# Loading the keys of the last unit but one in two halves (attention of one query row over a long cache, one core)

## The chip, the cores and the metric

The kernel runs on one core of one Trainium2 chip. The metric is the device time of one execution in microseconds (us), the median of several runs. Five engines work side by side, each with an instruction queue of its own: TensorE (PE in the profile, its weight loads PEld), VectorE (DVE), ScalarE (ACT), GpSimd (POOL) and SyncE (SP), which here only issues transfers between the main memory and the on-chip buffers (DMA). Engines and transfers meet through semaphores.

## The reference

Decoding attention with grouped queries: 32 query heads share 8 heads of keys and values. There is one query row for each head, and the cache is 65536 positions long with 128 numbers each, all in bf16. K and V hold 134 MB each and are read once.

```python
B, Hq, Hkv, Sq, Sk, D = 1, 32, 8, 1, 65536, 128
k = jnp.repeat(k, Hq // Hkv, axis=1)
v = jnp.repeat(v, Hq // Hkv, axis=1)
scores = jnp.einsum("bhqd,bhkd->bhqk", q, k) * D ** -0.5
p = softmax(scores, axis=-1)
return jnp.einsum("bhqk,bhkd->bhqd", p, v)
```

## The kernel before

**Units.** Each head of keys is cut into 4 units of 16384 positions, so there are NU = 32 units, numbered 0 to 31. A unit lies in a buffer as 128 partitions by T = 128 columns of 128 numbers, 32 KB in each partition and 4 MB in all. There are two buffers for keys, `kbuf[0]` for even and `kbuf[1]` for odd units, and one buffer `vbuf` that holds the values of two units.

**Rounds.** TensorE runs a loop of NR = 16 rounds of two units, a = 2i and b = 2i + 1: keys of a, keys of b, values of a, values of b. In the last round the values of b, unit 31, come after the loop, in `pe_last`.

**Keys** (`pe_keys`). The 128 columns are taken in G = 16 groups of 8. TensorE transposes the 8 columns of a group into one of four PSUM buffers `trb` (line 136). VectorE (line 229) or, for every fourth group, ScalarE (line 227) copies them to `ktb` in the on-chip memory. TensorE multiplies them with the 4 queries of the head into the scores `qkb` (line 147). The scores follow the transposes three groups behind (LAG = 3), so a unit opens with the transposes of four groups, 32 in a row. Before column 0 TensorE takes 16 from the semaphore `krdy` of the buffer, before column HALF = 64 it takes 16 from `khalf`:

```python
if t == 0:
    take(pe, krdy[b], 16)
if t == HALF:
    take(pe, khalf[b], 16)
```

**Softmax.** When the scores of a unit are done, VectorE finds their maximum over the columns (line 256), GpSimd the one over the partitions, VectorE the new running maximum, and ScalarE the exponentials `pts` (line 369), after which TensorE may use them.

**Values** (`value`, line 166). 128 multiplications of a column block of V with `pts` add up in `pvb`; VectorE adds the result to `acc`. After the second unit of a round VectorE increments `vfree` (line 310), which allows SyncE to fill `vbuf` again.

**The end** (`pe_last`). The values of unit 31 arrive in six pieces of 64, 32, 16, 10, 4 and 2 columns with a semaphore each. The first 126 columns go through line 166, in two runs of 64 and 62 that a small product (line 187) parts, the last two columns through line 196, and line 200 adds what was summed before. VectorE scales the result (line 357) and SyncE stores it (line 444).

**The order of the transfers.** SyncE issues everything in the order of its program: in round i the keys of unit 2i (after `kfree[0]`), those of 2i + 1 (after `kfree[1]`), then both units' values (after `vfree`). An eviction of the last group of a unit frees its key buffer. A unit's keys are one transfer that increments `krdy`; SyncE itself then adds 16 to `khalf` (lines 432 and 433), so that the wait at column 64 passes. For units 0 and 31 the keys are two transfers of 64 columns each, one increments `krdy`, the other `khalf` (line 430, with the issue in line 422). In the last round the values of unit 30 are one transfer (line 442), and those of unit 31 are the six pieces (line 443, issued by line 422).

## Time and profile before

| | |
|---|---|
| time, median of 3 runs | 633.53 us (633.5 to 633.71) |
| the profiled execution: time / span | 633.8 us / 632.0 us |
| mean granted clock of TensorE over the span | 0.789 |
| busy: PE / DVE / ACT / POOL | 77% / 49% / 29% / 3% |
| data read | 268.44 MB, 425 GB/s over the span |

The span runs from the first to the last instruction; the time has what lies around it as well. In rows of the timeline the first number is the start from the beginning of the span, the second the duration, both in us; merged rows stand for several instructions (x32). A bracket at the end of a row gives the idle time of that engine before it and what ended it; "PEq L41" means that TensorE's own queue released it, at the helper that waits for a semaphore (line 41). "SPq" are issues by SyncE's queue. "PEclk" is the share of full clock that TensorE was granted.

### The profile page before, as it was taken

How to read it: one execution, taken by the hardware profiler on the slowest of the kernel's cores; microseconds unless marked ns; L12 is line 12 of the kernel's file. 1: busy time of each engine (PE TensorE's matmuls, PEld its weight loads, DVE VectorE, ACT ScalarE, POOL GpSimd, SP SyncE). 2: the span in 40 equal slices, each digit the busy share in tenths (PEclk: the TensorE clock that was granted, in tenths of full speed). 3: DMA queues.
4: the chain of work that ended last, by engine and by line, in shares of the span. 5: the costliest groups of instructions: out<-in, count | busy, mean ns of one | idle time of the engine just before them, and what ended most of it. 6: DMA issues, size and time to landing. Idle time of an engine off the chain costs nothing. (4 is left out here: it accounts for less than half of the span.)

```text
span 632.0 us, 26791 instructions
## 1 busy us (share of the span) xinstructions
PE 489.4 (77%) x12294; PEld 482.3 (76%) x12294; DVE 312.0 (49%) x689; ACT 185.6 (29%) x410; POOL 15.9 (3%) x49
## 2 busy tenths in 40 slices
PE   4858869687796768968689497895968869687698
PEld 4858869687796768968689496885968869687697
DVE  4634627346272562725637165461744717356173
ACT  1321414214142240412414124141431414214142
POOL 0000000000000000000000000000000000000000
PEclk9866959769596895968969688695976959769596
DMA  8999999999999999999999999999999999999995
GB/s 367 450 418 444 428 425 442 433 446 419 431 448 415 448 415 431 448 415 448 415 431 452 413 450 417 450 428 417 450 423 456 415 431 452 417 450 412 417 431 203
DMA packets 8174, 268.61 MB, mean 425 GB/s; under 512 B 994, under 2 KB 1250, under 8 KB 1506
## 3 DMA queue, kind: packets, MB, share of 16 engines
q1 hardware_dynamic: 8072, 268.44, 98.7%
q8 instruction: 7, 0.11, 0.1%
q14 instruction: 5, 0.04, 0.0%
q10 hardware_dynamic: 90, 0.02, 0.0%
HBM read 268.44 MB, written 0.01 MB: 425 GB/s over the span
## 5 line engine op out<-in xcount | busy, mean ns | idle before, releaser
L136 PE MATMUL trb<-ident,kbuf 128*128 128x128 bf16 x4096 | 328.5, 233 | 41.3 <-PEq L41 41.3
L229 DVE COPY ktb<-trb 128x1024 bf16<-128x1024 bf16 x384 | 254.1, 689 | 101.0 <-PE trb L136 97.8
L136 PEld LDWEIGHTS trb<-ident,kbuf 128*128 128x128 bf16 x4096 | 263.1, 105 | 42.3 <-issue 42.2
L227 ACT ACTIVATE ktb<-trb 128x1024 bf16<-128x1024 bf16 x128 | 131.0, 1023 | 384.9 <-PE trb L136 324.8
L147 PE MATMUL qkb<-qcur,ktb 128*128 128x4 bf16 x4096 | 170.7, 165 | 22.7 <-PEq L41 21.9
L147 PEld LDWEIGHTS qkb<-qcur,ktb 128*128 128x128 bf16 x4096 | 153.2, 97 | 26.7 <-issue 23.9
L166 PE MATMUL pvb<-pts,vbuf 128*128 128x4 bf16 x4094 | 111.9, 166 | 71.6 <-PEq L41 68.7
L166 PEld LDWEIGHTS pvb<-pts,vbuf 128*128 128x128 bf16 x4094 | 110.8, 104 | 72.9 <-issue 72.9
L369 ACT ACTIVATE pts<-qkb,negm 128x128 bf16<-128x128 f32 x128 | 50.5, 540 | 0.9
L256 DVE TENSOR_REDUCE cmax<-qkb 128x4 f32<-128x512 f32 x32 | 22.1, 692 | 44.7 <-DVEq L41 43.7
L369 ACT ACTIVATION_READ_ACCUMULATOR pts<-qkb,negm 128x1 f32 x128 | 34.6, 270 | 0.0
L291 DVE TENSOR_TENSOR acc<-acc,pvb 128x4 f32<-128x4 f32 x23 | 3.6, 158 | 62.3 <-DVEq L41 62.3
L407 POOL PARTITION_ALL_REDUCE cmaxa<-cmax x32 | 11.9, 371 | 580.6 <-POOLq L41 580.6
L276 DVE TENSOR_TENSOR lp<-lp,alpha 128x4 f32<-128x4 f32 x24 | 3.8, 159 | 34.2 <-DVEq L41 34.2
L365 ACT ACTIVATE alpha<-dm 128x4 f32<-128x4 f32 x24 | 4.9, 205 | 52.6 <-ACTq L41 52.6
L289 DVE COPY acc<-pvb 128x4 f32<-128x4 f32 x8 | 1.3, 162 | 29.7 <-DVEq L41 29.7
L266 DVE TENSOR_TENSOR m<-m,cmaxa 128x4 f32<-128x4 f32 x24 | 3.8, 159 | 11.5 <-DVEq L41 11.5
L238 DVE COPY qcur<-qT 128x4 bf16<-128x4 bf16 x8 | 1.4, 170 | 11.8 <-DVEq L41 11.6
L283 DVE TENSOR_TENSOR acc<-acc,alpha 128x4 f32<-128x4 f32 x24 | 3.9, 163 | 4.2 <-DVEq L41 1.7
L267 DVE TENSOR_TENSOR dm<-m 128x4 f32<-128x4 f32 x24 | 3.9, 162 | 3.5
L277 DVE TENSOR_TENSOR lp<-lp,rsum 128x4 f32<-128x4 f32 x24 | 3.9, 162 | 3.5
L207 PE MATMUL trb<-ident,qsb 32*128 32x32 bf16 x1 | 0.2, 204 | 5.0 <-DMA qsb<-in_q_dram 5.0
(43 smaller groups left out, 26.8 us busy)
## 6 DMA issues: line engine op xcount, KB each, us to landing
kbuf<-in_k_dram SPq DMA_DIRECT2D x30, 4096.0 KB, 26.3
kbuf<-in_k_dram SPq DMA_DIRECT2D x4, 2048.0 KB, 16.0
vbuf<-in_v_dram SPq DMA_DIRECT2D x1, 4096.0 KB, 21.4
vbuf<-in_v_dram SPq DMA_DIRECT2D x1, 2048.0 KB, 26.0
vbuf<-in_v_dram SPq DMA_DIRECT2D x1, 1024.0 KB, 28.0
vbuf<-in_v_dram SPq DMA_DIRECT2D x1, 512.0 KB, 28.8
vbuf<-in_v_dram SPq DMA_DIRECT2D x1, 320.0 KB, 29.1
vbuf<-in_v_dram SPq DMA_DIRECT2D x15, 31.0
```

The source lines that it names most:

```text
L136: ins = pe.transpose(trb[j % NTB][:, i * P:(i + 1) * P], kv[:, t, :], ident[:, :])
L147: ins = pe.matmul(qkb[b][:, t * R:(t + 1) * R], lhsT=ktb[:, off:off + P], rhs=qcur[:, :], start=True, stop=True)
L166: return pe.matmul(pvb[b][:, 0:R], lhsT=vv[:, b * T + t, :], rhs=pts[b][:, t * R:(t + 1) * R], start=t == first, stop=t == last)
L227: ins = e.activation(dst, trb[j % NTB][:, :], AF.Copy).then_inc(eva, 1)
L229: ins = e.tensor_copy(dst, trb[j % NTB][:, :]).then_inc(evd, 1)
L256: e.tensor_reduce(cmax[:, :], qkb[u % 2][:, :].rearrange("p (t g) -> p g t", g=R), AX.X, ALU.max).then_inc(cm, 1)
L267: e.tensor_tensor(dm[:, :], mo[:, :], mn[:, :], ALU.subtract)
L277: own(e, e.tensor_tensor(lp[:, :], lp[:, :], rsum[:, :], ALU.add), xd)
L283: own(e, e.tensor_tensor(acc[:, :], acc[:, :], alpha[u % 2][:, :], ALU.mult), xd)
L365: e.activation(alpha[u % 2][:, :], dm[:, :], AF.Exp, scale=scale)
L369: ins = e.activation(pv[:, g, :], sv[:, g, :], AF.Exp, bias=negm[:, g:g + 1], scale=scale, accum_out=rsum[:, g:g + 1])
L407: e.partition_all_reduce(cmaxa[:, :], cmax[:, :], P, bass.bass_isa.ReduceOp.max).then_inc(cma, 1)
```

## The change

The condition in `load_k` that picks the units whose keys come as two transfers now names unit 30 (NU - 2) as well as 0 and 31:

```diff
             b = n % 2
             if n >= 2:
                 e.wait_ge(kfree[b], n // 2)
-            if n in (0, NU - 1):
+            if n in (0, NU - 2, NU - 1):
                 pieces(kbuf[b], src(kf, n), (HALF, T - HALF), (krdy[b], khalf[b]))
             else:
                 e.dma_start(kbuf[b][:, :], src(kf, n)).then_inc(krdy[b], 16)
                 e.sem_inc(khalf[b], 16)
```

For unit 30 one transfer of 4096 KB becomes two of 2048 KB, columns 0 to 63 and 64 to 127. The first increments `krdy[0]`, the second `khalf[0]`, and SyncE's own increment of `khalf[0]` is left out for this unit. Nothing else changes.

## The prediction

> **What bounds the kernel now.** I read the page first, then the list of DMA transfers, and last the merged timeline of the final 50 us. Two lines of the page say what rules most of the time:

> ```profile
> span 632.0 us, 26791 instructions
> q1 hardware_dynamic: 8072, 268.44, 98.7%
> ```

> The transfers of K and V keep the 16 DMA engines busy for 98.7% of the span. The change removes no bytes, so it can pay only where the program stops being held by the stream: at its end. The timeline of the end, rows of TensorE (PE), VectorE (DVE) and the SyncE queue (SPq); columns are start, duration, engine, line, operation, tiles, count, and in brackets the idle time before:

> ```profile
> 569.66 0.33 SPq L432 DMA_DIRECT2D kbuf<-in_k_dram  x1
> 580.94 0.81 SPq L422 DMA_DIRECT2D kbuf<-in_k_dram  x2
> 586.98 6.97 PE L166 MATMUL pvb<-pts,vbuf 128*128 128x4 bf16 x256 [4.48 <-PEq L41]
> 594.43 0.33 SPq L442 DMA_DIRECT2D vbuf<-in_v_dram  x1
> 594.80 2.81 SPq L422 DMA_DIRECT2D vbuf<-in_v_dram  x6
> 596.50 3.57 PE L136 MATMUL trb<-ident,kbuf 128*128 128x128 bf16 x32 [2.56 <-PEq L41]
> 603.00 0.61 PE L136 MATMUL trb<-ident,kbuf 128*128 128x128 bf16 x8
> 609.70 1.95 PE L136 MATMUL trb<-ident,kbuf 128*128 128x128 bf16 x32
> 621.24 3.55 PE L166 MATMUL pvb<-pts,vbuf 128*128 128x4 bf16 x128
> 625.46 1.85 PE L166 MATMUL pvb<-pts,vbuf 128*128 128x4 bf16 x64 [0.38 <-PEq L41]
> 627.36 1.82 PE L166 MATMUL pvb<-pts,vbuf 128*128 128x4 bf16 x62
> 629.11 0.37 PE L196 MATMUL pvb<-vbuf,pts 128*4 128x128 bf16 x2
> 630.05 0.34 DVE L357 TENSOR_SCALAR olast<-pvb,rl 4x128 bf16<-4x128 f32 x1 [0.68 <-PE pvb L200]
> ```

> Read downwards, this is: values of units 28 and 29 (586.98), a gap of 2.56 us, keys of unit 30 (596.50), keys of unit 31 (609.70), values of unit 30 (621.24), values of unit 31 in three rows (625.46, 627.36, 629.11), and the output. From 596.50 on TensorE and the engines that serve it hardly pause. To see whether that stretch waits for data, the issues are set beside the times to landing (last column, us from issue), first K of unit 30 and the two halves of K of unit 31, then V of unit 30 and the six pieces of V of unit 31:

> ```profile
> kbuf<-in_k_dram SPq DMA_DIRECT2D x1, 4096.0 KB, 26.7
> kbuf<-in_k_dram SPq DMA_DIRECT2D x1, 2048.0 KB, 20.3
> kbuf<-in_k_dram SPq DMA_DIRECT2D x1, 2048.0 KB, 24.8
> ...
> vbuf<-in_v_dram SPq DMA_DIRECT2D x1, 4096.0 KB, 21.4
> vbuf<-in_v_dram SPq DMA_DIRECT2D x1, 2048.0 KB, 26.0
> vbuf<-in_v_dram SPq DMA_DIRECT2D x1, 1024.0 KB, 28.0
> vbuf<-in_v_dram SPq DMA_DIRECT2D x1, 512.0 KB, 28.8
> vbuf<-in_v_dram SPq DMA_DIRECT2D x1, 320.0 KB, 29.1
> vbuf<-in_v_dram SPq DMA_DIRECT2D x1, 128.0 KB, 29.0
> vbuf<-in_v_dram SPq DMA_DIRECT2D x1, 64.0 KB, 28.7
> ```

> K of unit 30 lands at 569.66 + 26.7 = 596.4, some 0.1 us before its first transpose at 596.50: this landing ends the gap. K of unit 31 lands at 580.94 + 20.3 = 601.2 and 581.35 + 24.8 = 606.2 (the two issues fill 0.81 us, 0.41 each), before 609.70. V of unit 30 lands at 615.8, before 621.24. The six pieces are issued 0.476 us apart (2.81 us less a last issue of 0.43, over 5), from 594.80 to 597.18, and land at 620.8, 623.3, 624.6, 625.3, 625.7 and 625.9. They are used from 625.46, 627.4, 628.3, 628.8, 629.1 and 629.11 (29 ns for each column, from 62 in 1.82 us). Each is early; the last has the least to spare, 629.11 - 625.9 = 3.2 us. So the end of this kernel is a chain of TensorE work that starts with the landing of unit 30's keys and is not held by any later transfer.

> **The change, part by part.** *The first transpose of unit 30.* The keys arrive as two transfers of 2048 KB, and the first 64 columns release TensorE. The halves of unit 31 landed 606.2 - 601.2 = 5.0 us apart, so I put the first half of unit 30 at 596.4 - 5.0 = 591.4. TensorE is then still in the values of unit 29, which end at 586.98 + 6.97 = 593.95. What is late next is thus TensorE itself and the turn of its loop. That turn is seen uncovered once, in the second round, where the keys had long landed:

> ```profile
> 50.84 2.72 PE L166 MATMUL pvb<-pts,vbuf 128*128 128x4 bf16 x96 [2.85 <-issue]
> 53.61 3.57 PE L136 MATMUL trb<-ident,kbuf 128*128 128x128 bf16 x32
> ```

> From 53.56 to 53.61 are 0.05 us. The keys of unit 30 therefore start at 594.00 in place of 596.50: 2.50 us.

> *The second half.* TensorE now waits for a real landing at column 64, the first of the group of eight transposes at 603.00. That is 6.5 us after the start, so about 600.3 in the changed kernel, against a landing at 596.4: about 4 us to spare. Queued behind that wait are the other transposes of the unit, and behind them the evictions on VectorE and ScalarE; none is held.

> *The clock within unit 30.* TensorE starts these keys at half clock. The table of stretches (columns: stretch, length, busy time and count for PE, PEld, DVE, ACT, POOL, then PEclk, DMA share, GB/s) shows when it changes:

> ```profile
> 211.60:211.70 0.10, 0.10 (x6) 0.10 (x4) 0.09 (x1) 0.00 (x0) 0.00 (x0) 0.80 0.00 0
> 583.60:583.80 0.20, 0.00 (x0) 0.00 (x0) 0.00 (x0) 0.00 (x0) 0.17 (x1) 0.73 0.76 328
> 587.00:593.90 6.90, 6.90 (x256) 6.86 (x256) 0.48 (x3) 0.00 (x0) 0.00 (x0) 0.50 0.93 401
> 600.70:600.80 0.10, 0.10 (x4) 0.10 (x2) 0.00 (x0) 0.10 (x1) 0.00 (x0) 0.70 1.16 492
> 621.20:621.30 0.10, 0.10 (x7) 0.09 (x4) 0.00 (x0) 0.00 (x0) 0.00 (x0) 0.70 1.70 696
> ```

> A mean of 0.70 in 0.1 us between the levels 0.50 and 1.00 places an edge: up at 211.64, down at 583.69, up at 600.76, down at 621.24. The distances 17.07 and 20.48 are 5 and 6 times 3.414 us, so I read the edges as lying on a grid of that step. Unit 30 ran cold for 600.76 - 596.50 = 4.26 us. With a start at 594.00 the next grid point is 597.35, 3.35 us later. A round with almost that delay exists, unit 10, which starts at 208.24 and turns warm 3.40 us later; its rows, and the first one of unit 11:

> ```profile
> 208.24 3.55 PE L136 MATMUL trb<-ident,kbuf 128*128 128x128 bf16 x32 [2.59 <-PEq L41]
> ...
> 221.12 1.05 PE L136 MATMUL trb<-ident,kbuf 128*128 128x128 bf16 x16
> ```

> It takes 221.12 - 208.24 = 12.88 us from its keys to the next ones, where unit 30 took 609.70 - 596.50 = 13.20. That gives another 0.32 us, and a slope of 0.32 / 0.86 = 0.37 us for each us of cold time. If the grid lies otherwise in another execution, the delay can be as long as two steps, 6.8 us, which would cost 0.37 x 2.5 = 0.94 us instead: the gain lies between 1.6 and, with a delay a little shorter, 3.0.

> The row 587.00:593.90 holds more: TensorE is fully busy with values and stays at 0.50. [...]

> *The queue.* One more issue on SyncE, 0.41 us at 570.0, stands in front of nothing: the next, for unit 31, goes out at 580.94 when its buffer is free, and unit 30's own data land 26.7 us after the issue because other transfers are ahead. The increment of the second semaphore by SyncE goes away. The release of V's buffer comes from VectorE after the values of unit 29, which do not move, so V is issued at 594.43 as before. The price of the split on the stream is bounded by unit 31, whose halves took 606.2 - 596.4 = 9.8 us, and V of unit 30, one transfer, 615.8 - 606.2 = 9.6 us: up to 0.2 us later for V of unit 31. Below nothing there is no room, since the bytes are the same. I take 0.1.

> [...]

> *The sum.* 2.50 + 0.32 = 2.82 us, if nothing behind it is late. Keys of unit 31 start at 594.00 + 12.88 = 606.9, after both landings. Values of unit 30 start at 618.4, after 615.8. Values of unit 31 start at 622.6 (landed 620.8), reach column 64 at 624.5 (623.3), and the last two columns at 626.3, against 625.9 + 0.1. The stretch from 609.70 on moves as a whole, with 0.3 us left. The span goes from 632.0 to 629.2; the profiled execution took 633.8 us, 1.8 more than its span, and would take 631.0. The median of the three runs, 633.53, lies 0.27 below the profiled one, so the median of the changed kernel is 633.53 - 2.82 = 630.7 us.

> **The rivals.** [...]

> *The stream stops between the halves.* A transfer on an empty queue shows how long that could be:

> ```profile
> DMA to landing us min/median/max: 7.3/27.0/29.1
> ```

> The shortest landing of line 422 is 7.3 us, for 2048 KB that take 4.9 us in the stream (half of 9.8). The other 2.4 us are what would be lost if the second half only began when the first had been confirmed. V of unit 31 would then be complete at 628.3, 0.8 us before 629.11, so the gain shrinks to 0.8: 632.7 us. Against it stand the halves of unit 31, 5.0 us apart.

> *Nothing happens.* If the gap of 2.56 us were the turn of the loop, which the bracket <-PEq L41 (its own queue) does not exclude, an earlier landing would not start anything: 633.5. The same follows if the first half landed only with the second, by engines that do not keep to the order. Against these stand the 0.05 us at 53.56 and the halves of unit 31.

> *Slower.* The split halves the contiguous run of each partition. In the stretch where V's small pieces are moved the rate is low:

> ```profile
> 623.00:625.00 2.00, 2.00 (x69) 1.78 (x65) 0.24 (x3) 1.49 (x9) 0.00 (x0) 0.50 0.61 221
> ```

> At 221 GB/s the 4.19 MB of unit 30 would take 19.0 us instead of 9.7, and all later landings would move back by 9.3. The last piece of V would come at 635.2, 6.1 us after its use at 629.11: 639.6 us. This mechanism decides from a delay of 3.2 us on, below which V stays hidden even against the old end. Against it: unit 31 has runs of the same length and moves at the full rate.

> **How the numbers follow.** The forecast has a chance of 0.84, the warm clock 0.05, the stop between halves 0.04, nothing 0.05, slower 0.02. About 0.2%, 1.27 us, is what a measurement of this kernel can tell from no change. Forecast and warm clock are faster by more than that: 0.89. The stop (0.8 us) and nothing are within it: 0.09. Slower: 0.02. The range reaches down to the limit that the last piece of V sets, 630.3, and 0.1 for the spread of the runs: 630.2; upwards to a gain of 1.7, nearly the worst position of the clock's grid: 631.8.

> **What would show it.** In the changed profile two issues of 2048 KB stand near 569.7; the gap before the keys of unit 30 is about 0.05 us instead of 2.56; these keys start near 594.0, still at half clock, and turn warm near 597.4; keys of unit 31 start near 606.9 and the values of unit 30 near 618.4; the last piece of V still lands near 625.9 to 626.1, now just ahead of its use. Wrong would be: a gap that stays, a first half that lands after 594, V's last landing later by a microsecond or more, or an idle stretch of TensorE before the last columns.

## The result and the profile after

The changed kernel takes 630.88 us (median of 6 runs, 630.53 to 631.65) beside 633.71 us for the kernel before on the same chip (633.5 to 634.27): 2.83 us less, a ratio of 0.9956 with a 95% interval of 0.9943 to 0.9969. The profiled execution took 630.53 us with a span of 628.7 us; it is the fastest of the six. Its span and its main DMA queue:

```profile
span 628.7 us, 26791 instructions
q1 hardware_dynamic: 8216, 268.44, 99.2%
```

The bytes are the same, the packets 144 more: each of the 128 rows now comes in two packets, and 16 packets of 4 bytes are added. The timeline of the end, the rows that answer to those of the prediction:

```profile
569.35 0.81 SPq L422 DMA_DIRECT2D kbuf<-in_k_dram  x2
...
586.83 6.97 PE L166 MATMUL pvb<-pts,vbuf 128*128 128x4 bf16 x256 [4.65 <-PEq L41]
593.76 3.20 PE L136 MATMUL trb<-ident,kbuf 128*128 128x128 bf16 x32
...
594.65 2.81 SPq L422 DMA_DIRECT2D vbuf<-in_v_dram  x6
599.59 0.61 PE L136 MATMUL trb<-ident,kbuf 128*128 128x128 bf16 x8
606.28 1.95 PE L136 MATMUL trb<-ident,kbuf 128*128 128x128 bf16 x32
617.82 3.41 PE L166 MATMUL pvb<-pts,vbuf 128*128 128x4 bf16 x128
622.03 1.84 PE L166 MATMUL pvb<-pts,vbuf 128*128 128x4 bf16 x64 [0.52 <-PEq L41]
623.93 1.98 PE L166 MATMUL pvb<-pts,vbuf 128*128 128x4 bf16 x62
625.85 0.37 PE L196 MATMUL pvb<-vbuf,pts 128*4 128x128 bf16 x2
626.79 0.34 DVE L357 TENSOR_SCALAR olast<-pvb,rl 4x128 bf16<-4x128 f32 x1 [0.68 <-PE pvb L200]
```

The row at 593.76 has no bracket: the gap of 2.56 us before the keys of unit 30 is gone. These keys take 606.28 - 593.76 = 12.52 us to the next ones, against 13.20 before. The later stretches keep their lengths, 11.54 us for the keys of unit 31. Only the run of 62 columns at 623.93 has grown, from 1.82 to 1.98 us: it meets the landing of V. In the trace its products follow each other every 27 ns but for two late ones, columns 112 and 122, the first of two pieces of V: they start at 625.33 and 625.65, each 0.05 us after its piece has landed (625.28 and 625.60). The transfers, first the two halves of unit 30, then the last piece of V:

```profile
kbuf<-in_k_dram SPq DMA_DIRECT2D x1, 2048.0 KB, 22.1
kbuf<-in_k_dram SPq DMA_DIRECT2D x1, 2048.0 KB, 26.6
...
vbuf<-in_v_dram SPq DMA_DIRECT2D x1, 64.0 KB, 28.8
```

The halves land at 569.35 + 22.1 = 591.4 and at about 569.7 + 26.6 = 596.3, the last piece at 594.65 + 5 x 0.476 + 28.8 = 625.8. In the kernel before it landed at 625.9 with 3.2 us to spare; here line 196 uses it at 625.85, as it lands. Column 64 of unit 30, the first that needs the second half, is the row at 599.59: 3.3 us after that half has landed (about 4 were forecast), so the second wait costs nothing.

### The profile page after: what moved, and what is told of

It reads as the page before. It is cut to its first block, busy times and chain, and to the rows that moved or that the text cites. A ratio compares the mean times of both kernels' runs of the same rounds, so it can differ in the third digit from the quotient of the medians.

```text
span 628.7 us, 26791 instructions
## 1 busy us (share of the span) xinstructions
PE 487.7 (78%) x12294; PEld 480.6 (76%) x12294; DVE 311.9 (50%) x689; ACT 185.6 (30%) x410; POOL 15.9 (3%) x49
## 3 DMA queue, kind: packets, MB, share of 16 engines
q1 hardware_dynamic: 8216, 268.44, 99.2%
HBM read 268.44 MB, written 0.01 MB: 427 GB/s over the span
## 5 line engine op out<-in xcount | busy, mean ns | idle before, releaser
L136 PE MATMUL trb<-ident,kbuf 128*128 128x128 bf16 x4096 | 326.9, 232 | 39.2 <-PEq L41 39.1
L136 PEld LDWEIGHTS trb<-ident,kbuf 128*128 128x128 bf16 x4096 | 261.8, 104 | 40.1 <-issue 40.0
L147 PEld LDWEIGHTS qkb<-qcur,ktb 128*128 128x128 bf16 x4096 | 152.9, 97 | 26.7 <-issue 23.9
L166 PE MATMUL pvb<-pts,vbuf 128*128 128x4 bf16 x4094 | 111.9, 166 | 72.1 <-PEq L41 69.0
L166 PEld LDWEIGHTS pvb<-pts,vbuf 128*128 128x128 bf16 x4094 | 110.7, 104 | 73.5 <-issue 73.4
L256 DVE TENSOR_REDUCE cmax<-qkb 128x4 f32<-128x512 f32 x32 | 22.1, 691 | 44.7 <-DVEq L41 43.7
## 6 DMA issues: line engine op xcount, KB each, us to landing
kbuf<-in_k_dram SPq DMA_DIRECT2D x29, 4096.0 KB, 26.3
kbuf<-in_k_dram SPq DMA_DIRECT2D x6, 2048.0 KB, 21.4
vbuf<-in_v_dram SPq DMA_DIRECT2D x1, 4096.0 KB, 21.6
vbuf<-in_v_dram SPq DMA_DIRECT2D x1, 2048.0 KB, 26.1
vbuf<-in_v_dram SPq DMA_DIRECT2D x1, 1024.0 KB, 28.1
vbuf<-in_v_dram SPq DMA_DIRECT2D x1, 512.0 KB, 28.9
```

The costliest lines, as they stand in the source:

```text
L136: ins = pe.transpose(trb[j % NTB][:, i * P:(i + 1) * P], kv[:, t, :], ident[:, :])
L147: ins = pe.matmul(qkb[b][:, t * R:(t + 1) * R], lhsT=ktb[:, off:off + P], rhs=qcur[:, :], start=True, stop=True)
L166: return pe.matmul(pvb[b][:, 0:R], lhsT=vv[:, b * T + t, :], rhs=pts[b][:, t * R:(t + 1) * R], start=t == first, stop=t == last)
L256: e.tensor_reduce(cmax[:, :], qkb[u % 2][:, :].rearrange("p (t g) -> p g t", g=R), AX.X, ALU.max).then_inc(cm, 1)
```

## The experiments

Each kernel was timed against the kernel before on the same chip; intervals are 95%. The theory: the gain is the earlier start of unit 30's keys plus what the clock gives or takes, until the last piece of V sets the end. The main rival: the split itself helps, by way of the stream or the queue.

**The same split in the other order.** The half that releases TensorE is issued last. The edit against the kernel before:

```diff
-            if n in (0, NU - 1):
+            if n == NU - 2:
+                for lo, sm in ((HALF, khalf[b]), (0, krdy[b])):
+                    e.dma_start(kbuf[b][:, lo * D:(lo + HALF) * D],
+                                src(kf, n)[:, lo * D:(lo + HALF) * D]).then_inc(sm, 16)
+            elif n in (0, NU - 1):
```

> Unit 30 is loaded in the same two halves, with the same two semaphores, but the second half (columns 64 to 127) is issued first, so that the half that releases TensorE lands last, near 596.4 us. Theory (the gain comes from the earlier start of unit 30's keys alone): the keys start near 596.5 again, the gap of about 2.6 us is back, and the time is that of the kernel before, 633.7 us (within 0.4). Rival (the gain comes from the split of the transfer, in the stream or in SyncE's queue): 630.9 us, as in the changed kernel.

It took 633.97 us beside 633.85, ratio 0.9999 (0.999 to 1.0008). Its two transfers by time to landing, issued at 570.24 and 0.4 us later, and the first row of the keys:

```profile
kbuf<-in_k_dram SPq DMA_DIRECT2D x1, 2048.0 KB, 21.5
kbuf<-in_k_dram SPq DMA_DIRECT2D x1, 2048.0 KB, 26.0
...
596.77 3.57 PE L136 MATMUL trb<-ident,kbuf 128*128 128x128 bf16 x32 [2.67 <-PEq L41]
```

The first half to arrive, at 591.7, is of no use; the keys wait for the other one at 596.6, and the gap of 2.67 us is back. The split alone gains nothing.

**A larger first part.** Unit 30 as 112 and 16 columns, against the kernel before:

```diff
-            if n in (0, NU - 1):
+            if n == NU - 2:
+                pieces(kbuf[b], src(kf, n), (112, 16), (krdy[b], khalf[b]))
+            elif n in (0, NU - 1):
```

> Unit 30 is loaded as 112 and 16 columns instead of 64 and 64. Theory: the first part lands 3.7 us later than a first half does, near 595.1, so the keys start near 595.2, 1.3 us before those of the kernel before and 1.4 us after those of the changed one. Gain 1.3 us, plus or minus 0.6 for the position of the clock's grid: 632.4 us. Rival (the split itself, wherever it lies): 630.9 us. Rival (the second wait matters, its part landing at 596.4): no difference from the theory is expected, since column 64 is reached only near 601.

It took 632.78 us beside 633.85: 1.07 us less, ratio 0.9982 (0.9973 to 0.9991). The part of 3584 KB, issued at 569.15, and the keys:

```profile
kbuf<-in_k_dram SPq DMA_DIRECT2D x1, 3584.0 KB, 26.0
...
595.25 3.57 PE L136 MATMUL trb<-ident,kbuf 128*128 128x128 bf16 x32 [1.40 <-PEq L41]
608.15 1.95 PE L136 MATMUL trb<-ident,kbuf 128*128 128x128 bf16 x32
```

It lands at 595.1 and the keys start at 595.25, where they were expected. Of the earlier start, 2.66 us in the run of the changed kernel on the same chip (below), 1.25 us are left, and of its gain of 2.39 us 1.07 us are: 47% and 45%. The time follows the landing.

**The changed kernel again, twice.** Beside the run of the result there are two more with a profile each.

> The changed kernel once more, for the position of the clock's grid. Theory: the keys of unit 30 start between 593.7 and 594.1; the time from there to the keys of unit 31 is 12.52 us plus 0.37 us for each us that the clock turns warm later than 2.66 us after the start; the end follows it, but not below a span of 628.6 us, which the last piece of V sets. Median 630.9 us. Rival (the spread of the runs comes from the stream): the last piece of V lands later in longer executions, by as much as the span is longer.

> The changed kernel beside the run above. Theory (in executions in which the clock turns warm late, the chain of TensorE sets the end, in the others the last piece of V): its executions spread over 1.0 to 1.3 us, with the lowest near those of the run above.

They took 631.46 us (630.9 to 632.21, beside 633.85; ratio 0.9959, 0.9945 to 0.9972) and 631.57 us (630.96 to 631.85, beside 634.08; ratio 0.9961, 0.9948 to 0.9975): 2.39 and 2.51 us less than the kernel before. The median of the first was expected at 630.9 and is 0.6 above it; the spread of the second was expected at 1.0 to 1.3 and is 0.9. The keys of unit 30 and 31 and the last columns, of the first and then of the second:

```profile
593.84 3.57 PE L136 MATMUL trb<-ident,kbuf 128*128 128x128 bf16 x32
607.37 1.95 PE L136 MATMUL trb<-ident,kbuf 128*128 128x128 bf16 x32
626.79 0.37 PE L196 MATMUL pvb<-vbuf,pts 128*4 128x128 bf16 x2
```

```profile
593.93 3.57 PE L136 MATMUL trb<-ident,kbuf 128*128 128x128 bf16 x32
607.67 1.95 PE L136 MATMUL trb<-ident,kbuf 128*128 128x128 bf16 x32
627.07 0.37 PE L196 MATMUL pvb<-vbuf,pts 128*4 128x128 bf16 x2
```

and the stretches in which the clock rises, of the result's run, of the first and of the second (the column before the last two is PEclk):

```profile
596.30:596.50 0.20, 0.20 (x5) 0.20 (x4) 0.06 (x1) 0.00 (x0) 0.00 (x0) 0.69 0.57 246
```

```profile
598.90:599.10 0.20, 0.20 (x6) 0.20 (x4) 0.20 (x1) 0.00 (x0) 0.00 (x0) 0.77 1.16 492
```

```profile
599.40:599.60 0.20, 0.20 (x8) 0.20 (x6) 0.00 (x0) 0.00 (x0) 0.00 (x0) 0.74 0.77 328
```

| | keys start | clock rises | later by | keys take | last columns | span |
|---|---|---|---|---|---|---|
| result | 593.76 | 596.42 | 2.66 | 12.52 | 625.85 | 628.7 |
| again | 593.84 | 598.99 | 5.15 | 13.53 | 626.79 | 629.7 |
| again | 593.93 | 599.50 | 5.57 | 13.74 | 627.07 | 630.0 |

The same program starts the keys within 0.2 us of the same place, but the clock rises up to 2.9 us later, and the keys then take up to 1.2 us longer; that is 0.41 to 0.42 us for each us. The last piece of V landed at 625.8, 625.9 and 625.95, so the stream explains little of the spread. In the first execution V sets the end, in the other two the chain of TensorE does.

**The values of units 28 and 29 split as well.** TensorE is free earlier, so that the landing of the first half at 591.5 counts. The edit against the changed kernel:

```diff
-    vrdy = sem("vrdy")
+    vrdy, vrd1 = sem("vrdy"), sem("vrd1")
...
-        if b == 0:
-            take(pe, vrdy, 16)
+        take(pe, vrd1 if b else vrdy, 16)
...
-            if i < NR - 1:
+            if i < NR - 2:
                 e.dma_start(vbuf[:, :], src(vf, 2 * i, 2)).then_inc(vrdy, 16)
+                e.sem_inc(vrd1, 16)
+            elif i == NR - 2:
+                e.dma_start(vbuf[:, 0:T * D], src(vf, 2 * i)).then_inc(vrdy, 16)
+                e.dma_start(vbuf[:, T * D:2 * T * D], src(vf, 2 * i + 1)).then_inc(vrd1, 16)
```

> The changed kernel, and besides the values of units 28 and 29 as two transfers with a semaphore each, so that the values of unit 28 can start before those of unit 29 have landed. Theory: values of unit 28 near 582.5, those of unit 29 near 586.8 to 590.3, keys of unit 30 from the landing of their first half, near 591.5, about 2.3 us earlier than in the changed kernel. The chain then waits for the last pieces of V of unit 31, which still land near 625.8: span 628.5 to 628.7, time 630.4 us, in nearly every run whatever the clock's grid. Rival (the end is still set by the chain of TensorE, not by V): 630.9 - 2.3 = 628.6 us. Rival (the extra split holds up the stream): slower than the changed kernel, over 631 us.

> The kernel with unit 30's keys and the values of units 28 and 29 split, once more, beside the changed kernel on the same chip. Theory (its end is set by the last piece of V, not by the clock's grid): its executions lie within 0.5 us of each other and 0.5 us below the median of the changed kernel. Rival (it is no better): medians within 0.2 us.

It took 630.8 us (630.69 to 631.03, ratio 0.9949, 0.9936 to 0.9963) and, the second time, 630.72 us (630.58 to 630.88, ratio 0.9951, 0.9937 to 0.9965). Rows of the second:

```profile
581.82 3.37 PE L166 MATMUL pvb<-pts,vbuf 128*128 128x4 bf16 x128
587.01 3.56 PE L166 MATMUL pvb<-pts,vbuf 128*128 128x4 bf16 x128 [1.82 <-PEq L41]
591.76 3.57 PE L136 MATMUL trb<-ident,kbuf 128*128 128x128 bf16 x32 [1.19 <-PEq L41]
...
620.96 1.87 PE L166 MATMUL pvb<-pts,vbuf 128*128 128x4 bf16 x64 [0.98 <-DMA vbuf<-in_v_dram]
623.45 1.02 PE L166 MATMUL pvb<-pts,vbuf 128*128 128x4 bf16 x32 [0.51 <-DMA vbuf<-in_v_dram]
624.72 0.59 PE L166 MATMUL pvb<-pts,vbuf 128*128 128x4 bf16 x16 [0.24 <-DMA vbuf<-in_v_dram]
625.51 0.59 PE L166 MATMUL pvb<-pts,vbuf 128*128 128x4 bf16 x14 [0.20 <-DMA vbuf<-in_v_dram]
626.03 0.37 PE L195 MATMUL pvb<-vbuf,pts 128*4 128x128 bf16 x2
```

The keys start at 591.76, 2 us earlier than in the changed kernel, and the values of unit 31 now wait for V: at the first four pieces the brackets name the transfer, and the last columns at 626.03 start 0.06 us after the last piece has landed, at 625.97. The rival that TensorE's chain still sets the end would have given 628.6. My expectation of 630.4 us was 0.4 us too low, for the last piece landed at 626.29 in the first profiled execution and 625.97 in this one, not at 625.8, and the last columns run at 626.34 and 626.03; the spans, 629.2 and 628.9, stand 2.9 us behind them as in the table. This kernel was below the changed one on the same chip in both comparisons, by 0.7 and 0.9 us. The intervals of the ratios overlap; in the second comparison every execution of this kernel (at most 630.88) was shorter than every one of the changed kernel (at least 630.96). Its executions spread over 0.3 us in place of 0.9 to 1.3.

**The values split alone**, without the change to the keys (that edit, made in the kernel before).

> The kernel before (unit 30's keys whole) with only the values of units 28 and 29 as two transfers. Theory: the values are done earlier, near 590.5, but the keys of unit 30 still wait for the landing of the whole unit near 596.4, so the gap before them grows from 2.6 to about 6 us and the time does not fall: 633.8 us, within 0.4. Rival (TensorE's work before unit 30, not the landing, sets the end): 631.5 us or less.

It took 634.12 us beside 634.15, ratio 0.9999 (0.999 to 1.0008). Its keys of unit 30:

```profile
596.68 3.57 PE L136 MATMUL trb<-ident,kbuf 128*128 128x128 bf16 x32 [6.02 <-PEq L41]
```

The gap has grown to 6.02 us and the start has not moved: it is the landing of the keys that ends this gap, not TensorE's work nor the turn of its loop.

**The keys of every unit split.** The edit against the changed kernel:

```diff
-            if n in (0, NU - 2, NU - 1):
+            if True:
```

> The keys of every unit in two halves. Theory: in the rounds before the last the stream sets the pace, so an earlier start of the keys there is worth nothing, and a split costs the stream at most 0.1 us. Keys of unit 30 start near 593.8 plus what 29 further splits cost. Time between 631.2 (no price) and 634.1 us (0.1 each); the last landings move by the same amount. Rival (each split stops the stream for about 2.4 us): over 690 us. Rival (an earlier start is worth something in every round): under 630 us.

It took 633.48 us beside 634.15, ratio 0.999 (0.9981 to 0.9999): 0.67 us less than the kernel before, where the changed kernel had 2.39 to 2.83 us in its three comparisons. Values of units 28 and 29, keys of unit 30, and the last piece of V, with the row of its issues:

```profile
589.39 6.96 PE L166 MATMUL pvb<-pts,vbuf 128*128 128x4 bf16 x256 [8.63 <-PEq L41]
...
596.32 3.57 PE L136 MATMUL trb<-ident,kbuf 128*128 128x128 bf16 x32
597.22 2.81 SPq L422 DMA_DIRECT2D vbuf<-in_v_dram  x6
...
vbuf<-in_v_dram SPq DMA_DIRECT2D x1, 64.0 KB, 28.8
```

Against the changed kernel everything has moved back by 596.32 - 593.76 = 2.6 us, which is 0.09 us for each of 29 more splits, and the last piece lands at 628.4 in place of 625.8. The delay grows evenly: the values of the first round land 0.11 us later than in the changed kernel and those of the fourteenth 2.07, 0.08 us for each split, with a further 0.5 us in the fifteenth, whose cause stays open. An earlier start of the keys in the other rounds brought nothing that outweighs this. Issued by SyncE into a stream that fills 99.2% of the changed kernel's span, a further transfer moved the later landings by 0.09 us.

**No wait for the last values.** The kernel with both splits, its last products fed with the values of unit 30, which have long landed; the output of the last head is therefore not attention. The main part of the edit against the kernel with both splits:

```diff
-            ins = value(pe, b, t, 0, ROWS_FROM - 1)
-            if t in starts:
-                ins.wait_op(vpiece[starts.index(t)], 16, "sem-ge")
+            ins = pe.matmul(pvb[b][:, 0:R], lhsT=vv[:, t, :], rhs=pts[b][:, t * R:(t + 1) * R],
+                            start=t == 0, stop=t == ROWS_FROM - 1)
...
```

> The kernel with unit 30's keys and the values of units 28 and 29 split, in which the products of unit 31 read the values of unit 30 instead, which have long landed, so that nothing waits for the six pieces (they are still loaded, and SyncE waits for them after it has issued the last store). The output of the last head is therefore not attention. Theory (the six pieces set the end): values of unit 31 start near 620.4 without pauses, the last scaling on VectorE comes near 625.1 instead of 627.3, span near 627.0 to 627.4, time 628.6 to 629.2 us. Rival (the end is set by the chain of TensorE alone): 630.8 us as with the waits.

It took 628.85 us beside 634.15, ratio 0.992 (0.9906 to 0.9933), with a span of 627.0 us. The values of unit 31 and the last scaling:

```profile
620.43 1.85 PE L190 MATMUL pvb<-pts,vbuf 128*128 128x4 bf16 x64 [0.40 <-PEq L41]
...
625.02 0.34 DVE L353 TENSOR_SCALAR olast<-pvb,rl 4x128 bf16<-4x128 f32 x1 [0.68 <-PE pvb L196]
```

Without the waits the same chain ends 1.9 us earlier, with the scaling near the expected 625.1. So in the kernel with both splits the waits for the six pieces hold the end.

## Why the prediction was right, point by point

**The mechanism and the place held.** The gap before the keys of unit 30 was a wait for their landing: the reversed halves bring it back, the part of 112 columns moves it, and the values split alone lengthens it to 6.02 us. The rival of the loop's turn falls with these; so does that of the engines out of order, since the first half landed at 591.4 as forecast.

**The earlier start** was put at 2.50 us and measured 2.74 in the profiled pair. 0.15 of the difference is that the values of units 28 and 29 began 0.15 us earlier (586.83 for 586.98); the turn of the loop was 0.05 us in the forecast, and here the first transpose begins 0.04 us before the last value's modelled end.

**The clock** was put at 0.32 us and measured 13.20 - 12.52 = 0.68. This is the one term that was mis-sized. The step of the grid was right (3.414 us in the forecast, 13.65 / 4 = 3.413 in the changed kernel), but I took its position from the profile of before: the clock was to rise near 597.4 and rose at 596.42, 2.66 us after the start. The position differs from one execution to the next, as the bound of that paragraph allowed: 2.66, 5.15 and 5.57 us in three executions of one kernel. The slope came out at 0.41 to 0.42 us for each us instead of 0.37.

**The limit by V** was put at 3.2 us, with 0.3 to spare behind a gain of 2.82. In the profiled execution 2.74 + 0.68 = 3.42 us were there to gain, and the last columns moved by 629.11 - 625.85 = 3.26: the rest, 0.16 us, stands in the row of 62 columns, which took 1.98 us in place of 1.82. So this execution shows the limit itself, and the other two, with last columns at 626.79 and 627.07, show the chain.

**The agreement to 0.01 us is luck.** The forecast added 2.50 + 0.32 = 2.82; the profiled execution had 2.74 + 0.68 - 0.16 = 3.26, and the medians differ by 2.83. A likely reason is that the six executions hold both kinds, for their spans run from 628.7 to 629.9 us, but only one of them was profiled. In the two later comparisons the same change gained 2.39 and 2.51 us, 0.3 to 0.4 less than forecast. What the runs bear out is the mechanism, and a gain of 2.4 to 2.8 us.

**The price of the split** was taken as 0.1 us, between 0 and 0.2. The last piece of V landed no later in the changed kernel (625.8 to 625.95 for 625.9), and 29 further splits cost 0.09 us each. With that the rivals of a stop between the halves (2.4 us each) and of a slow half row (9.3 us) fall.

**A clock that is warm from the first key on**, 0.05 in the chances, did not come. The stretch of the values and that of the first transposes in the changed kernel:

```profile
587.00:593.70 6.70, 6.70 (x255) 6.70 (x252) 0.32 (x2) 0.00 (x0) 0.00 (x0) 0.50 1.01 430
593.80:596.40 2.60, 2.60 (x26) 2.60 (x27) 1.54 (x3) 0.00 (x0) 0.00 (x0) 0.50 0.96 410
```

TensorE is busy throughout, without a pause between the two, and the keys still start at 0.50.

## What to carry to other kernels

A kernel that its transfers hold for 99% of the time can still gain where the stream runs out: follow the last chain of work back from the end until a row has idle time before it, and ask which landing ended that idle. Then subtract the landing time of every later input from the time of its use: the smallest difference is the limit of what an earlier start can bring, here 3.2 us. A split had a price here, 0.09 us for each of 29 further ones, so it belongs at the one transfer that starts the last chain and not at all of them: at one unit the change gained 2.4 to 2.8 us, at every unit 0.7.

## What the runs showed of the hardware that I had not expected

The busy time that the profile counts does not tell when the clock rises. In the changed kernel 6.70 us of products with 4 columns, back to back, left the clock at 0.50, and 2.66 us into the transposes that followed, with nothing but transposes since (the first 32 run from 593.76 to 596.96), it rose at 596.42.

The whole profiles of the kernel before and of the changed kernel agree with this. Cut their stretches with the clock at 0.50 into steps of 3.413 us that end where it rises: each of the 32 steps with a rise at its end held at least 2.66 us of transposes (the least from 593.01 to 596.42 in the changed kernel), and each of the 117 without one at most 2.56 us (the most from 556.39 to 559.80 in the kernel before), though 31 of these were filled with products of values from end to end. Which property of the transposes counts was not shown; in the rows they have 128x128 numbers where the products have 128x4. The keys that open a round started cold in each of the 30 rounds from the second on in these two profiles, and the clock rose 2.66 to 5.97 us after their start. The two steps of 6.8 us in the prediction were an estimate; the longest delay measured in these 30 rounds is 5.97 us.
